# Retention and a gelu MLP on one core: earlier g sums, a seven-product first product from block 5 on, two more warm-ups and another hand-made order

## The chip, the cores and the metric

The kernel runs on one core of a Trainium2 chip. Its time is the device time of one execution in microseconds (us); lower is better. A core has TensorE (PE in the profile; PEld is its weight load), VectorE (DVE), ScalarE (ACT), GpSimd (POOL, which here only issues the load DMAs), SyncE (SP, which issues the stores and the transposing DMAs) and 16 DMA engines that all queues share.

## The reference

Retention for 8 batches, 8 heads, 576 positions and head size 64, then an MLP on the 4608 tokens that come out:

```python
scores = (q @ k.T) / sqrt(64)
Dmat[h] = where(i >= j, gamma_h ** (i - j), 0)      # gamma_h = 1 - 2 ** (-5 - h)
attn = (scores * Dmat) @ v                          # float32, [8, 8, 576, 64]
x = attn.transpose(0, 2, 1, 3).reshape(4608, 512)
h = x @ w_in                                        # 512 -> 2048
g = 0.5 * h * (1 + erf(h / sqrt(2)))
out = g @ w_out                                     # 2048 -> 512
```

Inputs and output are float32; the kernel multiplies in bfloat16.

## The kernel before, in words

**Attention.** Every batch is cut into five chunks of at most 128 positions (the fifth has 64), 40 chunks in all. For a chunk POOL loads q, k and v with a cast to bfloat16 (`load_chunk`, L247 and L251: from chunk 10 on, q and k go as two issues each). q and k are turned so that the head size lies on the partitions: the first 11 chunks with TensorE (`turn`, L343/L345, then a copy on DVE at L348 or ACT at L354), the others by a transposing DMA on SP (L332). A chunk then has: its v scaled by powers of gamma (`scaled_v`, DVE L432), scores on TensorE in 64 x 64 tiles (`together`, L382), a mask (`masked`: DVE L423 straight from PSUM, or ACT L421 first and then DVE), the inner product with v (`inner`, L458), a running state of the batch (`states`, L480 on TensorE, L489 to L498 on DVE and ACT), the cross product of q with that state (L382 again, into `o_ps`), and the write of x, transposed, by DVE (`evacuate`, L510). Work is done in groups: a group takes some *new* chunks up to their masked scores, and finishes the chunks that the group before had begun (the *held* ones). A chunk's x is therefore ready only with the group after its own.

**MLP.** Nine blocks of 512 tokens. Block t needs x of the chunks that cover its tokens: chunks 0 to 3 for block 0, to 8 for block 1, and so on for the later ones. Every block has a *first product* (h, then gelu on ACT into g) and a *second product* (g times w_out). All matmuls of both are issued at L320 (`product`). The tiles they write tell them apart in the profile: `hT` is the plain first product, 64 matmuls of 512 columns; `lean` is the first product by seven half-size products in place of eight (Strassen's scheme in Winograd's form), 4 groups x 7 x 4 matmuls of 256 columns; `fast` is the second product by seven products, 14 steps of 8 matmuls of 256 columns. A seven-product form needs sums of its operands beforehand: of g (`sum_g`, DVE L583 to L586, four slices S1 to S4 of a tile for each quarter of g), of w_out (`sum_weights`), of w_in (`sum_w_in`, L717 to L720, one of eight tiles at a time) and of x (`sum_x`, L734 to L737). And it combines the products: `lean` keeps two of them (L790 on ACT or L793 on DVE) and adds three times (DVE L797), before or between its gelus (L821).

`N_LEAN = 6` makes the first product of blocks 6, 7 and 8 `lean`; `N_DYN = 4` lets the first product of blocks 0 to 3 run on as many columns as have their x ("d" steps), while later blocks wait for all 512.

**The order.** No engine picks its work at run time. A planner in Python emits the instructions in one order for each engine, with a model clock for each engine, for PSUM banks and for the two DMA queues. It holds a list of *stages* and takes MLP steps only from the first stage that is not empty: first product of block 0; then first product of 1 with second of 0; then second of 1 with first of 2; and so on, and from the stage before the first `lean` block on, a lean first product together with the second product of the block before it. Between MLP steps it looks at what else can go (`attention_picks`): a group (G), scaling v (V), a turn (T), g sums (Z), late gelus (H), w_in sums (Y), x sums (X), w_out sums (W).

Groups come from `PLAN`. An entry is (number of new chunks, due, half-width). A group goes when `paced`, which counts 16 for each first or second product, has reached its due, or when the next MLP step is not ready for another 0.3 us of the model (*starved*). The third number says whether the full-array matmuls up to this group are issued as two half-width ones (`128*64` in the profile), so that the array need not change its tiling; two of these take the place of one `128*128`.

`LOADS` is the order in which POOL issues the first loads: a digit is a chunk (chunk 0 was loaded before), `i` the next of eight w_in tiles of 256 columns, `o` the next of eight w_out tiles. Afterwards chunk j + 10 is loaded when chunk j is done. w_in tile n serves rows 2n and 2n + 1 of the first product's 16. Other constants are margins of the planner: `V_SAFE` and `G_SAFE` (how long after the planned landing v is scaled, or a turned chunk is used), `Y_FROM` (from which `paced` on w_in sums may be made), `ACT_MASK` (how readily a mask goes by ACT), `T_LEAD`, `LAND_0`.

`sum_g` of block t is let go when the second product of block t - 1 has done 12 of its 14 steps, since the four slices are read up to then:

```python
if to_sum and fast_done.get(to_sum[0][0] - 1, 0) >= 12:
    got.append((g_ready(...) - 0.1, "Z", 0))
```

Before any MLP step is begun, the planner fills gaps of TensorE with matmuls of zeros (`warm`, L975); eight more stand at the very start (`warm_up`, L162).

Of the kernel before, what the change touches and what calls it, by code (L numbers as in the profile page):

```python
# [10 lines left out]
BF16 = mybir.dt.bfloat16  # L11
AF = mybir.ActivationFunctionType
ALU = mybir.AluOpType
# [3 lines left out]
def kernel(  # L17
# [14 lines left out]
    nc = tc.nc  # L32
# [11 lines left out]
    N_DF = d_ff // 128  # L44
# [6 lines left out]
    N_FIRST = 4  # L51
    N_LD = 7
    N_EX = 3
    Y_FROM = 88
    N_RING = 4
    LD_FIX = 2.0
    LD_TAIL = 1.7
    T_FIX = 2.1
    T_TAIL = 2.6
    T_DMA = 1.95  # L60
    N_DYN = 4
    N_LEAN = 6
    LEAN_FIRST = 1
    LOADS = "1 2 i 3 4 5 i 6 i i i 7 i i o i o o o 8 o o 9 o o"
    T_LEAD = 4
    V_SAFE = 4
    G_SAFE = 0
    TR_LEAD = 5
    POOL_0 = 1.05
    LAND_0 = (2.9, 4.15, 5.0)  # L70
    ACT_0 = 8.3
    COLS = ()
    CLOCK_0 = 3.2
    ACT_MASK = -0.2
    X_FROM = 10
    PLAN = [(1, 69, 1), (0, 67, 0), (0, 73, 0), (2, 142, 0), (1, 7, 1), (1, 119, 0), (2, 15, 0), (1, 61, 0), (2, 24, 0), (0, 26, 0), (0, 29, 0), (1, 0, 1), (2, 28, 0), (1, 58, 0), (2, 18, 0), (2, 29, 0), (0, 29, 0), (1, 21, 0), (2, 74, 0), (2, 99, 0), (2, 2, 0), (1, 47, 1), (2, 48, 0), (2, 106, 0), (2, 141, 1), (1, 154, 0), (2, 139, 0), (2, 69, 0), (2, 0, 1), (1, 68, 1), (0, 64, 1)]
    FAST_FROM = 0
    HALF = TOK_BLK // 2
    COL = d_model // 2
# [26 lines left out]
    clock = [0.0]  # L106
# [12 lines left out]
    def on_dve(ready, n, rate=1):  # L119
        return on("DVE", ready, n / rate / 960 + 0.072)  # L120
# [201 lines left out]
    def turn(i, parts=(0, 1)):  # L322

        cs = chunks[i][3]
        qk = loaded[i][0]
        s = st[i]
        if "qkT" not in s:
            s["qkT"] = tr_pool.tile([128, 2, HP, 128], BF16, tag="qkT", name="qkT")
            s["turned"] = 0.0
        qkT = s["qkT"]  # L330
        if i >= N_PE_TR:
            nc.sync.dma_start(qkT.rearrange("p j hp s -> p (j hp) s")[:, :, :cs],  # L332
                              qk[:cs].rearrange("p j h d -> p (j h d)"), transpose=True)
            transfer(1, clock[0] + T_FIX, T_DMA * cs / C, T_TAIL, s, "turned")
            return
        tiled(1 if by_col[0] and cs == C else 0)
        for j in parts:
            wait((land_q, land_k)[j][i] + 0.1)
            ps_, tag = bank([128, HP, 128], BF16, "qk_ps")
            for hp in range(HP):  # L340
                if by_col[0] and cs == C:
                    for e, sl in enumerate(HALVES):
                        nc.tensor.transpose(ps_[sl, hp, :cs], qk[:cs, j, 2 * hp + e, :], ident[:cs, :cs])  # L343
                else:
                    nc.tensor.transpose(ps_[:, hp, :cs], qk[:cs, j, 2 * hp:2 * hp + 2, :], ident[:cs, :cs])  # L345
            clock[0] += 0.23 * cs / C
            if i >= N_FIRST or i == 0:
                nc.vector.tensor_copy(qkT[:, j, :, :cs], ps_[:, :, :cs])  # L348
                end = on_dve(clock[0] + SEEN, HP * cs, 2)
                if i == 0 and j == 0:  # L350
                    nc.vector.tensor_scalar(msk[:, 0], row[:, :128], colp, None, op0=ALU.is_ge)
                    on_dve(end, 200)
            else:
                nc.scalar.copy(qkT[:, j, :, :cs], ps_[:, :, :cs])  # L354
                end = on_act(clock[0] + SEEN, HP * cs)
            free_at[tag] = end + BACK
            s["turned"] = max(s["turned"], end + BACK)
# [215 lines left out]
    w_sum_end = {0: 1e6, 4: 1e6}  # L573

    s_tiles = {}
    s_free = [0.0]

    def sum_g(t, n):

        g = g_tiles[t, n]  # L580
        a = {(r, c): g[:, :, c - 1, (r - 1) * HALF:r * HALF] for r in (1, 2) for c in (1, 2)}
        u = s_tiles[t, n] = s_pool.tile([128, 4, 2, HALF], BF16, tag=f"s{n}", name=f"s{n}")
        nc.vector.tensor_tensor(u[:, 0], a[2, 1], a[2, 2], op=ALU.add)  # L583
        nc.vector.tensor_tensor(u[:, 1], u[:, 0], a[1, 1], op=ALU.subtract)  # L584
        nc.vector.tensor_tensor(u[:, 2], a[1, 1], a[2, 1], op=ALU.subtract)
        nc.vector.tensor_tensor(u[:, 3], a[1, 2], u[:, 1], op=ALU.subtract)  # L586
        ready = max(s_free[0], g_ready(t, 0, TOK_BLK, range(4 * n, 4 * n + 4)))
        for x in range(4):
            s_end[t, n, x + 1] = on_dve(ready, 512, 2) + BACK

    def left(t, which, j, p):
# [343 lines left out]
    def attention_picks():  # L935
        got = []
        pend, i = held(), nxt["R"]
        pick = mlp_pick()
        kind, t = pick[1][0][:2] if pick is not None else ("s", N_BLK)
        starved = pick is None or pick[0] > clock[0] + 0.3  # L940

        if nxt["P"] < len(PLAN):
            size, due, _ = PLAN[nxt["P"]]
            new = list(range(i, i + size))
            if (paced[0] >= due or starved) and i + size <= nxt["T"]:
                got.append((group_ready(pend, new), "G", (pend, new)))
        i = nxt["V"]
        if i < nxt["T"] and i < nxt["S"] + 4:
            got.append((land_v[i] + (V_SAFE if i >= N_PE_TR else 0), "V", i))
        i = nxt["T"]  # L950
        if i < N_CH and i in land_v and i <= nxt["S"] + (T_LEAD if i < N_PE_TR else TR_LEAD):
            if i >= N_PE_TR:
                got.append((land_k[i], "T", i))
            elif i >= N_FIRST:
                got.append((max(land_k[i] + 0.1, banks_at(2)), "T", i))
            else:
                got.append((max((land_q, land_k)[half[0]][i] + 0.1, banks_at(1)), "T", i))
        if to_sum and fast_done.get(to_sum[0][0] - 1, 0) >= 12:
            got.append((g_ready(to_sum[0][0], 0, TOK_BLK, range(4 * to_sum[0][1], 4 * to_sum[0][1] + 4)) - 0.1, "Z", 0))
        if gelus:  # L960
            got.append((gelus[0][0] - 0.1, "H", 0))
        j = len(w_in_sums)
        if N_LEAN < N_BLK and j < len(w_in_sb) and not weights_due and paced[0] >= Y_FROM and nxt["S"] >= N_LD + N_EX:
            got.append((busy["DVE"] + 0.1, "Y", j))
        t = N_LEAN + len(x_sums)
        if t < N_BLK and j == len(w_in_sb) and (t == N_LEAN or lean_done.get(t - 1, 0) == 4 * len(FIRST_ORDER)) and x_ready(t * TOK_BLK, (t + 1) * TOK_BLK) < 1e5:
            got.append((max(busy["DVE"] + 0.1, x_ready(t * TOK_BLK, (t + 1) * TOK_BLK)), "X", t))
        if weights_due:
            got.append((weights_due[0][0], "W", 0))
        return got  # L970
# [6 lines left out]
    def attend(kind, i):  # L977
# [29 lines left out]
        elif kind == "V":  # L1007
            scaled_v(i)
            if i == 2:
                for t in ret_short + [vh_short]:  # L1010
                    nc.vector.memset(t, 0.0)
                    on_dve(clock[0], 256, 1.2)
            nxt["V"] += 1
        elif kind == "H":
            gelu_late()
        elif kind == "Y":
            sum_w_in(i)
        elif kind == "X":
            sum_x(i)
        elif kind == "Z":  # L1020
            sum_g(*to_sum.pop(0))
        elif kind == "W":
            sum_weights(*weights_due.pop(0)[1:])
        elif i < N_FIRST:
            turn(i, (half[0],))
            nxt["T"] += half[0]
            half[0] = 1 - half[0]
        else:
            turn(i)
            nxt["T"] += 1  # L1030
# [4 lines left out]
    def mlp(run):  # L1035
        step = run.pop(0)
        kind, t = step[:2]
        if kind == "d":
            m = step[2]
            lo, hi = reach(t, m)  # L1040
            if hi - lo < 64:
                hi = lo + 64
            done[t, m] = hi
            mlp1_step(t, m, lo, hi)
            cost = (hi - lo) / TOK_BLK
            if hi < TOK_BLK:
                run.append(step)
            else:
                for other in stages:
                    for r in other:  # L1050
                        if step in r:
                            r.remove(step)
        elif kind == "1":
            mlp1_step(*step[1:])
            cost = 1.0
        elif kind == "f":
            lean_step(*step[1:])
            lean_done[t] = lean_done.get(t, 0) + 1
            cost = 4.0 / len(FIRST_ORDER)
        else:  # L1060
            fast_step(t, step[2])
            fast_done[t] = step[2] + 1
            if step[2] == 11:
                s_free[0] = clock[0] + SEEN
            cost = 16 / len(FAST_ORDER)
        paced[0] += cost

# [51 lines left out]
```

## Time and profile before

| | |
|---|---|
| median of 6 runs | 289.58 us (288.21 to 291.76) |
| profiled execution | 289.64 us |
| its span, first to last instruction | 287.9 us |
| mean granted TensorE clock | 0.994 |
| POOL, which issues the loads, is last busy in | slice 26 of 40 (to 187 us) |
| first w_in sums / last | 108.6 us / 170.7 us |
| x sums of blocks 6, 7, 8 | 183.1, 213.1, 240.5 us |
| first second-product matmul | 50.47 us |
| last group of attention | 216.9 us |

The first lines of the page give each engine's busy time over the span, then the span in 40 slices of 7.2 us, where a digit is the busy share in tenths. An answer by stages gives, for each stretch, its length, the busy time of each engine with its number of instructions, the granted TensorE clock, the mean share of the DMA engines (over 1 when packets queue) and GB/s. The chain of waits runs from the last instruction back to what released it; its rows are start, length, engine, tile and number of instructions.

### The profile page before, as it was taken

To read this page: it belongs to the slowest core of one execution; us is meant where nothing else is said; L and a number is where in the kernel's file an instruction comes from. 1 tells how busy PE (TensorE), PEld (TensorE's weight loads), DVE (VectorE), ACT (ScalarE), POOL (GpSimd) and SP (SyncE) were. 2 spreads that over 40 slices of the span, in tenths; PEclk is the share of its full clock that TensorE was granted. 3 is DMA by queue.
4 is the path that set the end of the run, shared out by engine and by line. 5 is a ranking of instruction groups with operands and counts; after the bars stand their busy time and mean duration, and the time that the engine had idled before them with its cause. 6 is when DMAs were issued, how large, how long until landed. Compare 5 with 4: busy or idle time off the path is not lost.

```text
span 287.9 us, 8831 instructions
## 1 busy us (share of the span) xinstructions
PE 277.4 (96%) x3671; PEld 215.4 (75%) x3671; DVE 222.0 (77%) x553; ACT 152.2 (53%) x309; POOL 147.3 (51%) x198
## 2 busy tenths in 40 slices
PE   6769999999998999999999999999999999999995
PEld 2457557998887578656875588558999888888884
DVE  7888865874986895799779888998867965975552
ACT  3836576634425742576246723577662585467321
POOL 8987758998778369877968797300000000000000
PEclk9989999999999999999999999999999999999999
DMA  9999999999999999999999999990101210220223
GB/s 132 155 158 173 196 187 160 119 143 191 143 126 184 189 162 156 182 175 134 171 193 160 165 139 149 131 145 2 39 2 42 72 36 2 75 75 0 75 73 109
DMA packets 157319, 35.43 MB, mean 123 GB/s; under 512 B 141920, under 2 KB 157280, under 8 KB 157280
## 3 DMA queue, kind: packets, MB, share of 16 engines
q0 software_dynamic: 117792, 18.10, 96.3%
q1 hardware_dynamic: 39488, 16.78, 32.0%
q8 instruction: 28, 0.46, 0.7%
q14 instruction: 11, 0.09, 0.1%
HBM read 36.70 MB, written 9.44 MB: 160 GB/s over the span
## 4 chain that ended last, share of the span: by engine, by line
PE 89%; DMA 5%; POOL 3%; DVE 1%; issue 1%; ACT 0%; DVEq 0%; ACTq 0%; POOLq 0%
PE fast L320 37%; PE hT L320 30%; PE lean L320 13%; PE sc L382 3%; DMA qkT<-qk_ld 3%; PE o_ps L458 3%; DMA v_ld<-in_v_dram 2%; POOL qk_ld L251 2%; PE u_ps L480 2%; PE o_ps L382 1%; PE qk_ps L345 1%; POOL v_ld L251 1%; DVE ret L423 0%; POOL v_ld L128 0%; POOL w_in L262 0%
## 5 line engine op out<-in xcount | busy, mean ns | idle before, releaser
L320 PE MATMUL hT<-xT,w_in 128*64 128x512 bf16 (+8 forms) x624 | 88.9, 334 | 1.0 <-DVE xT L510 0.8
L320 PEld LDWEIGHTS <-w_in 128*128 128x128 bf16 (+1 forms) x816 | 62.8, 103 | 34.8 <-issue 1.0
L552 ACT ACTIVATE g<-hT 128x512 bf16<-128x512 f32 (+6 forms) x129 | 61.3, 490 | 30.7 <-PE hT L320 28.7
L320 PEld LDWEIGHTS <-s 128*128 128x128 bf16 (+1 forms) x616 | 56.5, 99 | 6.7 <-DVE s L584 0.3
L320 PE MATMUL fast<-w_sum,s 128*128 128x256 bf16 (+1 forms) x472 | 50.8, 273 | 0.0
L247 POOL DMA_DIRECT2D qk_ld<-in_q_dram x60 | 44.9, 777 | 11.4 <-DMA qkT<-qk_ld 8.1
L247 POOL DMA_DIRECT2D qk_ld<-in_k_dram x60 | 44.3, 761 | 10.0 <-DMA v_ld<-in_v_dram 6.0
L320 PEld LDWEIGHTS <-g 128*128 128x128 bf16 (+1 forms) x464 | 42.2, 100 | 5.5
L251 POOL DMA_DIRECT2D v_ld<-in_v_dram x39 | 35.0, 897 | 6.6 <-DVE o L675 1.8
L320 PE MATMUL fast<-w_out,g 128*128 128x256 bf16 (+1 forms) x320 | 33.4, 273 | 0.0
L671 ACT COPY u<-fast 128x512 f32<-128x512 f32 (+1 forms) x20 | 10.8, 542 | 37.0 <-PE fast L320 37.0
L675 DVE TENSOR_TENSOR o<-fast,u 128x512 f32<-128x512 f32 (+1 forms) x20 | 12.7, 633 | 19.4 <-ACT u L671 9.7
L510 DVE TENSOR_TENSOR xT<-o_ps,dq 128x256 bf16<-128x256 f32 (+1 forms) x84 | 26.5, 373 | 0.3 <-PE o_ps L382 0.3
L423 DVE TENSOR_TENSOR ret<-sc,msk 128x512 bf16<-128x512 f32 x39 | 25.0, 682 | 1.1 <-PE sc L382 0.8
L432 DVE TENSOR_TENSOR vh<-v_ld,dv 128x512 bf16<-128x512 bf16 x32 | 21.7, 680 | 1.8 <-DMA v_ld<-in_v_dram 1.8
L797 DVE TENSOR_TENSOR m<-lean,m 128x512 f32<-128x512 f32 x24 | 16.4, 687 | 6.8 <-PE lean L320 4.0
L583 DVE TENSOR_TENSOR s<-g 128x512 bf16<-128x512 bf16 x36 | 15.0, 417 | 5.2 <-ACT g L552 4.2
L382 PE MATMUL sc<-qkT 64*64 64x128 bf16 (+1 forms) x576 | 15.7, 218 | 1.6 <-DMA qkT<-qk_ld 0.9
L320 PE MATMUL fast<-w_sum,g 128*128 128x256 bf16 x144 | 17.2, 273 | 0.0
L320 PE MATMUL fast<-w_out,s 128*128 128x256 bf16 x144 | 17.2, 272 | 0.0
L821 ACT ACTIVATE g<-m 128x512 bf16<-128x512 f32 x24 | 14.9, 631 | 4.1 <-DVE m L797 4.1
L584 DVE TENSOR_TENSOR s<-s,g 128x512 bf16<-128x512 bf16 x36 | 15.3, 425 | 1.2
(93 smaller groups left out, 369.8 us busy)
## 6 DMA issues: line engine op xcount, KB each, us to landing
out_dram<-o SPq DMA_DIRECT2D x32, 256.0 KB, 4.2
v_ld<-in_v_dram POOLq DMA_DIRECT2D x32, 128.0 KB, 6.2
qk_ld<-in_q_dram POOLq DMA_DIRECT2D x50, 64.0 KB, 6.0
qk_ld<-in_k_dram POOLq DMA_DIRECT2D x50, 64.0 KB, 5.2
w_in<-in_moe_w_in_dram POOLq DMA_DIRECT2D x8, 256.0 KB, 8.2
w_out<-in_moe_w_out_dram POOLq DMA_DIRECT2D x8, 256.0 KB, 8.7
out_dram<-o SPq DMA_DIRECT2D x8, 128.0 KB, 1.7
qk_ld<-in_q_dram POOLq DMA_DIRECT2D x7, 128.0 KB, 6.0
```

The costliest lines, as they stand in the source:

```text
L247: nc.gpsimd.dma_start(dst[:cs, HP * odd:HP * odd + HP], src[b, odd::2, c0:c0 + cs, :].rearrange("h s d -> s h d"))
L251: nc.gpsimd.dma_start(dst[:cs], src[b, :, c0:c0 + cs, :].rearrange("h s d -> s h d"))
L320: nc.tensor.matmul(out_[sl], lhsT=lhsT[:, sl], rhs=rhs, start=start, stop=stop, skip_group_check=True)
L382: nc.tensor.matmul(out_, lhsT=lhsT, rhs=rhs, start=start, stop=stop, skip_group_check=True)
L423: nc.vector.tensor_tensor(r[:cs, :, :cs], src, msk[:cs, :, :cs].to_broadcast([cs, HP, cs]), op=ALU.mult)
L432: nc.vector.tensor_tensor(vh[:cs], loaded[i][1][:cs], dv[:cs, :, ci:ci + 1].to_broadcast([cs, H, D]), op=ALU.mult)
L510: nc.vector.tensor_tensor(xT[:, g::2, at:at + hi - lo], s["o_ps"][g][:, s["place"], :, lo:hi], dq[:, g::2, c0 + lo:c0 + hi], op=ALU.mult)
L552: nc.scalar.activation(g_of(t, m, lo, hi), hT[:, :hi - lo], AF.Gelu)
L583: nc.vector.tensor_tensor(u[:, 0], a[2, 1], a[2, 2], op=ALU.add)
L584: nc.vector.tensor_tensor(u[:, 1], u[:, 0], a[1, 1], op=ALU.subtract)
L797: nc.vector.tensor_tensor(dst, acc_, f[to], op=ALU.add)
L821: nc.scalar.activation(g_tile(t, n)[:, :, r - 1, lo:lo + HALF], src, AF.Gelu)
```

## The change

- `sum_g` is split: the sums into slices 1, 2 and 3 of block t are let go after 10 steps of the second product of t - 1 (those slices are read in steps 5 to 10), the one into slice 4 after 12 steps, by a new pick "E" that comes ahead of "Z". The four sum tiles are allotted once and no longer taken anew from a pool for each block.
- `N_LEAN` goes from 6 to 5, `N_DYN` from 4 to 3.
- Two warm-up matmuls of 512 columns are issued after chunk 0's q is turned.
- `LOADS`, `PLAN` and the margins are other ones.

```diff
-    Y_FROM = 88
+    Y_FROM = 20
...
-    N_DYN = 4
-    N_LEAN = 6
+    N_DYN = 3
+    N_LEAN = 5
     LEAN_FIRST = 1
-    LOADS = "1 2 i 3 4 5 i 6 i i i 7 i i o i o o o 8 o o 9 o o"
-    T_LEAD = 4
-    V_SAFE = 4
-    G_SAFE = 0
+    LOADS = "1 i 2 3 4 5 6 i i 7 i i i 8 i i 9 o o o o o o o o"
+    T_LEAD = 5
+    V_SAFE = 1
+    G_SAFE = 0.5
...
-    LAND_0 = (2.9, 4.15, 5.0)
+    LAND_0 = (2.9, 4.3, 5.0)
...
-    ACT_MASK = -0.2
+    ACT_MASK = 0.3
     X_FROM = 10
-    PLAN = [(1, 69, 1), (0, 67, 0), (0, 73, 0), (2, 142, 0), (1, 7, 1), (1, 119, 0), (2, 15, 0), (1, 61, 0), (2, 24, 0), (0, 26, 0), (0, 29, 0), (1, 0, 1), (2, 28, 0), (1, 58, 0), (2, 18, 0), (2, 29, 0), (0, 29, 0), (1, 21, 0), (2, 74, 0), (2, 99, 0), (2, 2, 0), (1, 47, 1), (2, 48, 0), (2, 106, 0), (2, 141, 1), (1, 154, 0), (2, 139, 0), (2, 69, 0), (2, 0, 1), (1, 68, 1), (0, 64, 1)]
+    PLAN = [(1, 528, 0), (1, 321, 0), (1, 269, 1), (2, 27, 0), (2, 99, 0), (2, 135, 0), (1, 17, 0), (1, 4, 1), (1, 19, 0), (1, 0, 0), (2, 24, 0), (2, 48, 0), (1, 43, 0), (1, 32, 1), (2, 85, 0), (2, 39, 0), (2, 22, 0), (2, 52, 0), (2, 125, 0), (0, 109, 0), (1, 77, 0), (2, 27, 0), (0, 82, 1), (1, 128, 1), (1, 112, 0), (1, 81, 1), (1, 124, 1), (0, 6, 1), (2, 160, 1), (2, 56, 1), (0, 71, 1)]
...
                 if i == 0 and j == 0:
+                    warm(2)
                     nc.vector.tensor_scalar(msk[:, 0], row[:, :128], colp, None, op0=ALU.is_ge)
...
-    s_free = [0.0]
-
-    def sum_g(t, n):
+    s_free = [0.0, 0.0]
+    to_end = []
+
+    s_sb = [s_pool.tile([128, 4, 2, HALF], BF16, name=f"s{n}") for n in range(N_DF // 4)]
+
+    def sum_g(t, n, last):
...
-        u = s_tiles[t, n] = s_pool.tile([128, 4, 2, HALF], BF16, tag=f"s{n}", name=f"s{n}")
+        u = s_tiles[t, n] = s_sb[n]
+        if last:
+            nc.vector.tensor_tensor(u[:, 3], a[1, 2], u[:, 1], op=ALU.subtract)
+            s_end[t, n, 4] = on_dve(s_free[1], 512, 2) + BACK
+            return
...
-        nc.vector.tensor_tensor(u[:, 3], a[1, 2], u[:, 1], op=ALU.subtract)
         ready = max(s_free[0], g_ready(t, 0, TOK_BLK, range(4 * n, 4 * n + 4)))
-        for x in range(4):
+        for x in range(3):
...
-        if to_sum and fast_done.get(to_sum[0][0] - 1, 0) >= 12:
+        if to_end and fast_done.get(to_end[0][0] - 1, 0) >= 12:
+            got.append((clock[0], "E", 0))
+        if to_sum and fast_done.get(to_sum[0][0] - 1, 0) >= 10:
             got.append((g_ready(to_sum[0][0], 0, TOK_BLK, range(4 * to_sum[0][1], 4 * to_sum[0][1] + 4)) - 0.1, "Z", 0))
...
-            sum_g(*to_sum.pop(0))
+            to_end.append(to_sum[0])
+            sum_g(*to_sum.pop(0), False)
+        elif kind == "E":
+            sum_g(*to_end.pop(0), True)
...
-            if step[2] == 11:
-                s_free[0] = clock[0] + SEEN
+            if step[2] in (9, 11):
+                s_free[step[2] // 11] = clock[0] + SEEN
```

## The prediction

> **What bounds the kernel now.** I read the page first (busy shares, then the slices), then the busy time by stage, then the chain, then the first 43 us on TensorE, VectorE and the load queue.
>
> ```profile
> PE 277.4 (96%) x3671; PEld 215.4 (75%) x3671; DVE 222.0 (77%) x553; ACT 152.2 (53%) x309; POOL 147.3 (51%) x198
> PE   6769999999998999999999999999999999999995
> DVE  7888865874986895799779888998867965975552
> PEclk9989999999999999999999999999999999999999
> DMA  9999999999999999999999999990101210220223
> ```
>
> TensorE is busy everywhere but in the first three slices (7.2 us each) and in slice 13; the DMA engines are full for the first 27 slices. So the end is the start-up, plus TensorE's work, plus a tail. Stages (PE, PEld, DVE, ACT, POOL busy, clock, DMA share, GB/s):
>
> ```profile
> 9.00:19.20 10.20, 6.47 (x163) 4.52 (x162) 8.36 (x20) 6.57 (x15) 9.46 (x13) 1.00 2.29 157
> 19.20:27.15 7.95, 7.82 (x141) 6.32 (x140) 6.90 (x19) 3.43 (x11) 7.05 (x9) 0.79 1.80 172
> 27.15:43.00 15.85, 15.85 (x134) 8.80 (x132) 12.22 (x32) 11.00 (x22) 10.25 (x14) 1.00 1.65 188
> 60.00:100.00 40.00, 39.13 (x517) 31.40 (x515) 29.94 (x70) 17.18 (x37) 30.14 (x41) 1.00 1.90 163
> 165.00:197.00 32.00, 32.00 (x465) 22.33 (x465) 27.43 (x72) 15.94 (x31) 15.68 (x22) 1.00 1.46 129
> ```
>
> From 19.2 us on TensorE stands still for 0.13 + 0.87 us, and 0.13 more near 250 us. The 0.87 is one wait for a DMA transpose at 88.0 us. The clock of 0.79 in the second row is one record of half clock, 19.39 to 22.80 us, with TensorE busy: about 1.7 us lost. The chain gives prices per matmul, and VectorE shows what the start hangs on:
>
> ```profile
> 266.35 18.35 PE fast L320 x168
> 204.12 7.04 PE lean L320 x128
> 187.74 7.03 PE hT L320 x64
> ```
> ```profile
> 11.89 0.69 DVE L432 TENSOR_TENSOR vh<-v_ld,dv 128x512 bf16<-128x512 bf16 x1 [1.03 <-DMA v_ld<-in_v_dram]
> 16.61 0.69 DVE L432 TENSOR_TENSOR vh<-v_ld,dv 128x512 bf16<-128x512 bf16 x1 [0.80 <-DMA v_ld<-in_v_dram]
> ```
>
> 18.35/168 = 109.2 ns for 256 columns. The 64 hT rows are half-width pairs: 7.03/32 = 0.220 us for 512 columns; at full width the chain has 28 in 6.04 us, 0.2157 each. VectorE stands waiting for the v of chunk 2 and of chunk 3: start-up is paced by landings, one about every 0.9 us.
>
> **The Trainium skill.** TensorE: Matmul & The Clock Gate, "What's actually happening": the array runs at half clock after a window of some 3.4 us with little activity. The trace agrees: the half-clock record is 3.413 us long and follows a stretch where TensorE was busy 6.47 of 10.20 us. Same page, "Wait — 56ns, not 53.3ns?": N/2.4 + 2.5 ns, 109.2 ns at 256 columns; the trace has 109.2. VectorE: DVE Perf Modes, "The perf-mode tier table": tensor_tensor runs at double rate on bf16 in SBUF, at single rate with float32 or PSUM; here 418 ns (s) against 687 ns (m<-lean,m), both of 512 columns.
>
> **The change, part by part.**
>
> *Seven products for block 5.* Out go 64 matmuls of 512 columns, 64 x 0.2157 = 13.80 us. In come 4 groups x 7 products x 4 matmuls of 256: 112 x 0.1092 = 12.23. TensorE: -1.6 us (-1.8 if the old ones ran half-width). It lies on the path, as TensorE never rests there. Beside it VectorE gains 12 adds x 0.69 = 8.3 and four x sums x 0.418 = 1.7; the 8 keeps go to ACT mostly (20 of 24 did), 8 x 0.59 = 4.7 there.
>
> *Is VectorE cover enough?* By counting units before it (16 per product), block 5's first product would share its stage with block 4's second, from about 165 us. That stage has VectorE at 27.43 of 32.00. Of the eight w_in sums (4 x 0.285 = 1.1 us each) two stand here, at 169.8 and 170.7 us; they move to before 70 us, where VectorE has room: -2.3. The four x sums at 183 stay, for block 5 in place of 6. 27.4 - 2.3 + 8.3 = 33.4 us in some 30.4: over by 3.0. The mask constant moves masks to ACT (414 ns on VectorE in place of 682): a third of some 9 saves 0.8. The rest can be put off until after 197 us, where VectorE is at 16.21 of 20.00. Bounds: 0 to +3; I take +0.3.
>
> *The g sums.* Same four operations, 36 of each at 418 ns; only their start moves. Waits for fast matmuls before L583 are 1.0 us in three, on VectorE, and weight loads wait 0.3 us for s in all. TensorE has other products while they run: 0, bounds -0.3 to +0.3.
>
> *Two warm-ups.* They fall between 5.24 and 6.23 us, where TensorE waits 1.00 us for k's cast; at 0.43 us each they need 0.86. Cover gone, +0.4; taken 0.
>
> *Safety margins.* v may be scaled 3 us sooner after its planned landing. From chunk 11 on, where the margin holds, VectorE scales v at the least 2.0 us after it landed (chunk 12, at 62.5 us), else at the least 4.0 (chunks 20, 21, 28): one wait of 1 us may come on VectorE, with masks and x queued behind it, while TensorE has matmuls that need neither; 0, upper bound +1. A group of attention waits 0.5 us longer for its transposes: the 0.87 us stall at 88.0 may go, or come back elsewhere. -0.4, bounds -0.9 to +0.5.
>
> *Load order.* Bytes are unchanged and the last w_out lands at 50.2 us either way, so the first second product (at 50.47) keeps its start; POOL has the same issues, and from chunk 10 on the loads follow as before. In between I shift the landings of before by what goes ahead: chunk 2.8 us, w_in tile 1.3. w_in 0: 13.4 to 10.4; chunk 2: 11.9 to 13.3; chunk 3 stays at 16.6; w_in 1 (the second): 21.9 to 25.5; w_in 3 and 4 +2.5 us, 6 +2.5, 7 +1.2; chunk 6 lands 1.4 earlier, 7 and 8 about 2.7 and 8. Block 1's first product can't begin before block 0's is whole, since the planner looks at the first stage alone. So until 25.5 us TensorE has from weights only w_in 0: 2 x 0.87 us.
>
> *The list there.* New groups are chunks 1; 2; 3+4; 5+6; 7+8; 9. A chunk's x comes with the next group. x of chunk 2 thus waits for chunk 4 (landed 18.7), x of chunk 3, which completes block 0, for chunk 6 (24.2): about 27 us, against 19.5 to 24 now. TensorE from 19.5 to 25.3 then has group 3+4 (1.2 us), a 128-column piece of two tiles (0.4), transposes of 5 and 6 (0.9), half of group 5+6 (0.8): 3.3 of 5.8 us, idle 2.5. From 25.5 on, tiles 2 to 5 with the rest of 0 and 1 and chunk 7's transposes fill up to 29.9; w_in 3 lands at 30.7: idle 0.8. Tiles 6 to 11 fill up to 36; w_in 6 lands at 37.3, less chunk 8's transposes: idle 0.8. Together 4.1. Credit: 0.4, as one more 128-column piece falls before 19 us; and the half clock of before, 1.7 us, would lie under idle time now, but can return when work resumes: I take half, 0.8. +2.9, bounds -1.7 (other attention fills every hole and the clock does not drop) and +5.4 (no clock credit, and one half-clock window of 3.4 us on resumed work).
>
> *Other.* 31 list entries each; two more do something (31 against 29), at some 0.3 us; three more half-width stretches save as many switches. 0.
>
> Sum: 287.9 - 1.6 + 0.3 - 0.4 + 2.9 = 289.1 span. The profiled execution took 289.64, 1.7 outside its span: 290.8. Its time stands 0.06 above the median of the runs, so 290.8 is also the forecast against 289.58: +0.4%.
>
> **Rivals.**
> A, the forecast: the early hole eats the saving. 290.8; its own range 287.7 to 292.4.
> B, slower: half clock on the resumed work. Place: 25.5 to 30 us. The window before it has TensorE busy about half, less than the stretch that brought the dip of before. Price: early term +5.4 for +2.9, 293.3. It decides once the early loss passes 4.6 us. Against: the warm-ups at 5 us don't reach it, but TensorE's many small matmuls count too, and the stretch 9 to 16 us had no dip.
> C, faster: the hole is filled. Attention of chunks 5 and 6 done singly is not in the list, but its pieces may be spread; no dip; the 0.87 goes. -1.6 - 0.9 - 1.7 = -4.2: 285.4. Against: before 25.5 us one w_in tile is there and nothing else can be multiplied.
> D, VectorE becomes the bound from 165 to 197: +3.0 in place of 0.3, 293.5; if half is made up after, 292. For: 33.4 in 30.4. Against: the second product of block 4 (12.2 us) asks VectorE for only three adds and is there to fill.
> That the change does not do what it says I leave at nothing: the first product of a block is one of two forms, and 5 is named.
>
> **How the numbers follow.** A 0.58, all within 1%. B 0.22, all slower. C 0.10: 0.09 faster, 0.01 within. D 0.10: half slower, half within. About 1% (2.9 us) is what a measurement here can tell from nothing. Faster 0.09, same 0.64, slower 0.27. Range: A's lower end, set a little down for C's nearest part, 287.2, up to B and most of D, 294.0; left out are most of C and the far ends. A's own range stands above.
>
> **What would show it.** In the new profile: lean matmuls 448 full-width equivalents, not 336, and hT 320 for 384; TensorE's busy time between 19.2 and 43 us down by 2 to 4 us, with idle before w_in tiles or chunk 6's transposes; w_in sums before 70 us; the last group of attention near 217 us less 1.6 plus the early loss; fast from 266 us on unchanged. A half-clock record after 25 us speaks for B; VectorE over 95% from 165 to 197 with TensorE waiting for m or s speaks for D. I am wrong if TensorE is as full at 19 to 43 us as now, or if new idle time stands in the middle.

## The result, and the profile after

The changed kernel takes 290.15 us (median of 34 runs, 288.67 to 292.65), the kernel before 289.28 us (69 runs beside it, 287.13 to 293.27). The ratio is 1.0041, 95% interval 1.0027 to 1.0055: 1.2 us slower, where 290.8 against 289.58, also 1.2 us, was forecast. The profiled execution took 289.66 us with a span of 287.9, as long as that of the kernel before (289.64 and 287.9), so these two executions don't show the difference: that of the kernel before lies 0.4 us above its median, that of the changed kernel 0.5 us under its own. What they show, stage by stage, is where the saving is spent again.

The page after, busy shares and slices:

```profile
PE 278.8 (97%) x3992; PEld 220.8 (77%) x3992; DVE 231.0 (80%) x575; ACT 155.5 (54%) x311; POOL 147.2 (51%) x198
PE   8779999999999999999999999999999999999995
DVE  7699687688957896899959799599789877997732
PEclk9986999999999999999999999999999999999999
DMA  9999999999999999999999999942202101120223
```

VectorE has 9.0 us more, close to the 9.2 that the prediction's terms add up to (8.3 + 1.7 - 0.8). TensorE looks fuller in slices 1 and 3. In slice 1 stand the two new warm-ups; in slices 3 and 4 its clock has an 8 and a 6. The same stages as before:

```profile
9.00:19.20 10.20, 7.09 (x146) 4.81 (x146) 7.48 (x18) 6.58 (x15) 9.99 (x13) 1.00 2.70 152
19.20:27.15 7.95, 7.33 (x145) 6.12 (x140) 7.43 (x19) 2.81 (x8) 7.14 (x10) 0.57 2.33 166
27.15:43.00 15.85, 15.85 (x176) 9.28 (x175) 12.24 (x33) 11.22 (x25) 11.87 (x17) 1.00 1.63 189
60.00:100.00 40.00, 39.86 (x527) 30.27 (x527) 32.10 (x82) 16.08 (x32) 31.55 (x43) 1.00 2.01 168
165.00:197.00 32.00, 32.00 (x496) 28.56 (x494) 26.98 (x60) 21.33 (x42) 15.06 (x21) 1.00 1.42 130
```

In the second row the clock is 0.57: the record has half clock from 19.75 to 26.58 us, two windows where the kernel before had one. TensorE is "busy" for 7.33 of 7.95 us there because the little it has takes twice as long. The mean clock hides idle time, and busy time hides half clock, so I counted work instead: every matmul that has begun, at the measured prices (109.2 ns for 256 columns, 215.7 ns for 512, and on the straight line through these two for other widths), halved for half-width and quartered for 64 x 64 tiles, warm-ups left out. The *lag* is the time less the work begun until then, that is, what TensorE has lost so far to waits, to half clock and to small pieces. What the seven products save is no part of the lag; it is in the total of the work:

| at us | lag before | lag after | after less before |
|---|---|---|---|
| 19.2 | 14.60 | 14.48 | -0.1 |
| 27.15 | 17.11 | 18.86 | +1.8 |
| 43 | 17.81 | 19.62 | +1.8 |
| 80 | 19.94 | 21.61 | +1.7 |
| 100 | 22.07 | 22.75 | +0.7 |
| 165 | 24.93 | 26.37 | +1.4 |
| 197 | 26.51 | 27.74 | +1.2 |
| 284 | 27.45 | 29.06 | +1.6 |

The work itself fell by 1.72 us: hT 83.2 to 69.3, lean 36.7 to 48.9, all else as before. So the changed kernel has 1.7 us less to do, and is 1.8 us behind from its start-up on. What it regains from 80 to 100 us is mostly one wait of the kernel before that it doesn't have:

```profile
88.00 0.42 PE L382 MATMUL sc<-qkT 64*64 64x128 bf16 x16 [0.87 <-DMA qkT<-qk_ld]
```

The chain gives the same prices as before: 109.2 ns for 256 columns at full width, 54.5 ns at half width, and 219 ns for 512 columns, where the kernel before, too, has a row of 32 in 7.01 us:

```profile
268.86 15.73 PE fast L320 x144
206.49 4.80 PE lean L320 x88
128.23 7.01 PE hT L320 x32
```

VectorE's longest early wait is no longer for v of chunk 2 or 3, but for scores; the v's have landed when it comes to them. Chunk 2's v landed at 13.34 us and is scaled at 16.87, so it is the list that holds it up:

```profile
11.93 1.29 DVE L424 TENSOR_TENSOR ret<-sc,msk 128x512 bf16<-128x512 f32 x2 [1.45 <-PE sc L383]
16.87 0.68 DVE L433 TENSOR_TENSOR vh<-v_ld,dv 128x512 bf16<-128x512 bf16 x1
18.29 0.63 DVE L433 TENSOR_TENSOR vh<-v_ld,dv 128x512 bf16<-128x512 bf16 x1
```

### The profile page after: what moved, and what is told of

Same layout as the page of the kernel before. It is cut to its first block, busy times and chain, and to the rows that moved or that the text cites. A ratio compares the mean times of both kernels' runs of the same rounds, so it can differ in the third digit from the quotient of the medians.

```text
span 287.9 us, 9521 instructions
## 1 busy us (share of the span) xinstructions
PE 278.8 (97%) x3992; PEld 220.8 (77%) x3992; DVE 231.0 (80%) x575; ACT 155.5 (54%) x311; POOL 147.2 (51%) x198
## 4 chain that ended last, share of the span: by engine, by line
PE 86%; DVE 8%; ACT 3%; DMA 1%; issue 1%; SPq 0%; DVEq 0%; ACTq 0%
PE fast L320 36%; PE hT L320 22%; PE lean L320 17%; PE sc L383 3%; PE o_ps L459 3%; PE u_ps L481 2%; DMA k<-in_k_dram 1%; PE o_ps L383 1%; DVE xT L511 1%; DVE ret L424 1%; ACT dq L169 1%; DVE s L588 1%; PE qk_ps L345 1%; DVE vh_short L433 1%; DVE s L592 1%
## 5 line engine op out<-in xcount | busy, mean ns | idle before, releaser
L320 PEld LDWEIGHTS <-w_in 128*128 128x128 bf16 (+1 forms) x764 | 56.8, 104 | 33.2 <-DVE xT L511 1.7
L320 PE MATMUL hT<-xT,w_in 128*128 128x512 bf16 (+8 forms) x468 | 73.8, 343 | 1.4 <-DVE xT L511 1.3
L553 ACT ACTIVATE g<-hT 128x512 bf16<-128x512 f32 (+4 forms) x99 | 49.8, 517 | 22.6 <-PE hT L320 21.7
L804 DVE TENSOR_TENSOR m<-lean,m 128x512 f32<-128x512 f32 x32 | 21.8, 686 | 5.4 <-PE lean L320 4.7
L828 ACT ACTIVATE g<-m 128x512 bf16<-128x512 f32 x32 | 20.1, 631 | 8.7 <-DVE m L804 8.5
L424 DVE TENSOR_TENSOR ret<-sc,msk 128x512 bf16<-128x512 f32 x30 | 19.7, 684 | 3.2 <-PE sc L383 2.3
L496 ACT CAST u_sb<-run_sum 128x256 bf16<-128x256 f32 x24 | 9.7, 405 | 22.7 <-DVE run_sum L493 17.8
L320 PEld LDWEIGHTS <-w_in_sum 128*64 128x64 bf16 (+1 forms) x288 | 20.2, 106 | 1.4 <-issue 0.2
L320 PE MATMUL lean<-x_sum,w_in_sum 128*64 128x256 bf16 (+1 forms) x216 | 19.9, 273 | 0.0
L422 ACT CAST ret<-sc 128x512 bf16<-128x512 f32 x34 | 18.3, 585 | 2.7 <-PE o_ps L383 2.7
```

Source lines behind the costliest of these rows:

```text
L320: nc.tensor.matmul(out_[sl], lhsT=lhsT[:, sl], rhs=rhs, start=start, stop=stop, skip_group_check=True)
L422: nc.scalar.copy(r[:cs, :, :cs], src)
L424: nc.vector.tensor_tensor(r[:cs, :, :cs], src, msk[:cs, :, :cs].to_broadcast([cs, HP, cs]), op=ALU.mult)
L553: nc.scalar.activation(g_of(t, m, lo, hi), hT[:, :hi - lo], AF.Gelu)
L804: nc.vector.tensor_tensor(dst, acc_, f[to], op=ALU.add)
L828: nc.scalar.activation(g_tile(t, n)[:, :, r - 1, lo:lo + HALF], src, AF.Gelu)
```

## The experiments

The theories: (1) the early feed of w_in and the pairing of chunks eat what the seven products save; (2) the half clock costs the time; (3) VectorE can't carry block 5's extra adds, and the saving is given back as waits. Ratios are against runs of the kernel before on the same chip, with 95% intervals.

**The load order of before in the changed kernel** (`after_loads_before`).
```diff
-    LOADS = "1 i 2 3 4 5 6 i i 7 i i i 8 i i 9 o o o o o o o o"
+    LOADS = "1 2 i 3 4 5 i 6 i i i 7 i i o i o o o 8 o o 9 o o"
```


> The changed kernel with the load order of before. If the early feed of w_in is what eats the saving (theory 1), useful TensorE work by 43 us rises by about half of the 1.8 us that it lies behind, since the list of groups still pairs chunks 3+4 and 5+6: 289.2 us against 290.15. If the half clock alone costs the time (theory 2), it stays within 0.4 us unless the granted clock rises. If VectorE in the lean stage is the cause (theory 3), 290.1.


297.37 us, ratio 1.0305 (1.0268 to 1.0342): a miss, but a telling one. At 35 us the lag is 16.50, 2.4 us better than in the changed kernel (at full clock here, which was worth 1.1 at 27 us) and 1.3 better than before (17.79, with one half-clock window): this load order does feed TensorE. Then the list asks for chunks 7 and 8 together, and chunk 8 now lands after four w_out tiles. TensorE's waits from 35 to 50 us:

```profile
40.44 0.40 PE L345 MATMUL qk_ps<-ident,qk_ld 128*128 128x128 bf16 x4 [2.88 <-DMA qk_ld<-in_q_dram]
41.20 0.61 PE L345 MATMUL qk_ps<-ident,qk_ld 128*128 128x128 bf16 x4 [0.37 <-DMA qk_ld<-in_k_dram]
45.56 0.29 PE L345 MATMUL qk_ps<-ident,qk_ld 64*128 64x64 bf16 x4 [1.03 <-DMA qk_ld<-in_q_dram]
46.46 0.29 PE L345 MATMUL qk_ps<-ident,qk_ld 64*128 64x64 bf16 x4 [0.61 <-DMA qk_ld<-in_k_dram]
```

Two half-clock windows, from 40.86 and 47.69 us, come with these waits. At 60 us it lags by 26.51, 5.9 us worse than the changed kernel. List and load order are one decision.

**The load order of the changed kernel in the kernel before** (`before_loads_after`), the same edit the other way.


> The kernel before with the load order of the changed one alone. Theory 1, early feed: useful TensorE work at 27 us falls back by about 1.5 us, as in the changed kernel (1.75), and stays lost: 290.6 to 291.3 against 288.9. If it is the pairing of chunks in the list that costs the time, not the loads: 289.3 or less.


296.41 us, ratio 1.0256 (1.0212 to 1.0300). At 27 us it lags 1.0 us more than before, at 43 us 2.3 more (20.11 against 17.81): an early loss comes with the loads alone, though the old list takes chunks 3 and 4 singly. How much of it is half clock is not separated here: the run has two windows, from 15.58 to 22.41 us, where the kernel before has one. The rest comes at 94.5 us, where TensorE waits 3.3 us for a DMA transpose, probably again a list that doesn't fit its loads; the total is thus no measure of the early step.

**Block 5 by seven products alone** (`before_lean5`).
```diff
-    Y_FROM = 88
+    Y_FROM = 20
-    N_LEAN = 6
+    N_LEAN = 5
```


> The kernel before with the seven-product first product from block 5 on, and its w_in sums let go from 20 units of work on; nothing else. Theory 1: it saves what TensorE saves, 1.7 us, so 287.6 against 289.3. Theory 3: VectorE can't keep up from 165 to 197 us, TensorE waits for m or s, and the time stays at 289.3 or goes over it.


298.36 us, ratio 1.0356 (1.0317 to 1.0394). Up to 197 us nothing is given back: its lag is 24.95 against 26.51 of the kernel before, even 1.6 us less. (This is not the saving, which the lag leaves out; the wait at 88 us, 0.87 us, is gone here.) Then it loses 12 us until 255. TensorE's waits from 214 to 256 us in its timeline:

```profile
224.76 4.78 PE L320 MATMUL fast<-w_sum,s 128*64 128x256 bf16 x84 [1.78 <-DVE s L584]
239.78 1.92 PE L320 MATMUL lean<-x_sum,w_out 128*64 128x256 bf16 x16 [3.50 <-DVE x_sum L736]
252.83 0.60 PE L320 MATMUL lean<-x_sum,w_in_sum 128*128 128x256 bf16 x4 [1.63 <-DVE lean L797]
```

These waits are 6.9 us of it, and a half-clock window from 239.23 us comes with the longest. VectorE is not full (16.93 of 23.00 us from 217 to 240): it comes late with what TensorE asks for next. The last group of attention, at 217 us before, comes at 246 here, so x of the last blocks, and the x sum at 238.5 us, come when the seven-product steps already wait for them. The old list doesn't hold for the new mix of work: TensorE does wait for VectorE, as theory 3 says, though not because VectorE lacks time.

**Block 5 plain again in the changed kernel** (`after_lean6`).
```diff
-    N_LEAN = 5
+    N_LEAN = 6
```


> The changed kernel with block 5's first product plain again, list and all else kept. If the seven products save TensorE's 1.7 us under this list (theory 1), it comes out 1.7 us slower than the changed kernel: 291.8. If they give back what they save as waits for VectorE (theory 3), it stays at 290.1.


292.12 us, ratio 1.0127 (1.0095 to 1.0158), against 1.0041 for the changed kernel: 2.5 us slower, 1.5 to 3.5 by the two intervals. In the profile its lag at 284 us is 28.90 (changed kernel 29.06), so up to there nothing but the work differs, by 1.72 us, and TensorE's last matmul ends 1.4 us later (285.99 against 284.58). Another 1.4 us of this one execution is its last store, which landed 3.12 us after its issue, in the changed kernel 1.70. Under its own list the saving is real and is not given back: theory 3 falls for the changed kernel.

**All four g sums after 12 steps** (`after_sums_whole`).
```diff
-        if to_sum and fast_done.get(to_sum[0][0] - 1, 0) >= 10:
+        if to_sum and fast_done.get(to_sum[0][0] - 1, 0) >= 12:
```


> The changed kernel with its first three g sums let go after 12 steps of the second product of the block before, as the fourth, and not after 10. The prediction's step says 0, 0.3 at most: 290.1. If the seven products of block 5 leave so little room on VectorE that the sums must be early (theory 3), TensorE waits for s or m between 190 and 240 us and several us are lost, 294 or more.


298.98 us, ratio 1.0371 (1.0337 to 1.0404). At 180 us it is 1.7 us ahead of the changed kernel (lag 24.95 against 26.62), at 240 it is 8.3 behind. VectorE's timeline, then TensorE's:

```profile
197.60 0.43 DVE L592 TENSOR_TENSOR s<-s,g 128x512 bf16<-128x512 bf16 x1
197.95 0.42 DVE L593 TENSOR_TENSOR s<-g 128x512 bf16<-128x512 bf16 x1
198.28 0.42 DVE L588 TENSOR_TENSOR s<-g,s 128x512 bf16<-128x512 bf16 x1
198.62 0.42 DVE L490 COPY run_sum<-u_ps 128x256 f32<-128x256 f32 x1
```
```profile
199.09 3.14 PE L320 MATMUL fast<-w_out,g 128*64 128x256 bf16 x30 [3.58 <-DVE run_sum L490]
```

From 192.77 to 198.62 us VectorE makes sixteen sums in a row. Behind them stands the copy of the running state out of PSUM (L490), and the next second product, which needs no sum at all, waits for it: 3.58 us. That the two share a PSUM bank is inferred from this wait; the records do not name banks. A second wait, 2.70 us for an addition of the output on VectorE, follows at 225.6, and half-clock windows from 198.41 and 229.13 us come with the two. The time is the one expected under theory 3, but the waits are not for `s` or `m`: what VectorE does is in the wrong order for TensorE. In the changed kernel twelve sums run from 192.50 to 197.01 and the last four, apart, from 198.68; there TensorE has no wait in this stretch.

**The split alone in the kernel before** (`before_split_sums`): the diff of the change in `sum_g` and its picks, nothing else.


> The kernel before with the split of the g sums alone: three after 10 steps, the fourth after 12, sum tiles allotted once. The prediction's step says 0, 0.3 at most: 288.6 to 289.3. If starting the sums earlier puts them ahead of masks and x on VectorE that attention waits for, 290 to 291.


290.51 us, ratio 1.0083 (1.0054 to 1.0112), slower by more than the changed kernel, and in the range expected if the early sums stand ahead of what attention needs. It has a wait of the same kind in another place, at 70.6 us:

```profile
72.48 2.69 PE L320 MATMUL fast<-w_out,g 128*128 128x256 bf16 x23 [1.88 <-DVE run_sum L492]
```

It also gives a pair: neither this profile nor that of `after_sums_whole` has a half-clock record before 190 us. At 43 us their lags are 16.14 and 18.72, so with the old and the new start compared at full clock, the new one is 2.6 us behind. Here the busy time shows the hole as well, first the old start (`before_split_sums`), then the new one (`after_sums_whole`):

```profile
19.20:27.15 7.95, 7.85 (x147) 5.83 (x146) 7.74 (x22) 4.94 (x14) 7.93 (x11) 1.00 1.83 176
```
```profile
19.20:27.15 7.95, 6.09 (x149) 4.60 (x144) 7.92 (x21) 3.49 (x10) 7.33 (x10) 1.00 2.22 166
```

TensorE stands idle for 1.9 us in this stretch with the new start and for 0.1 with the old one; from 27.15 to 43 us both are full. `after_loads_before` makes a third: it has the new list and the old loads, and no half clock before 40 us. At 27.15 us the three lags are 15.60 (old), 16.59 (new list, old loads) and 17.72 (new), at 35 us 16.06, 16.50 and 17.79. So the loads make 1.1 of 2.1 us and then 1.3 of 1.7, and the rest is the list's with its margins, in one execution each.

**Filled gaps** (`after_warm_fill`, `before_warm_fill`).
```diff
-        if gap > 0.4 and not mlp_begun[0]:
+        if gap > 0.28 and (not mlp_begun[0] or clock[0] < 25):
```


> The changed kernel with TensorE's planned gaps of over 0.28 us before 25 us of the planner's clock filled with matmuls of zeros, also after the first MLP step. Theory 1: the half clock lies mostly under idle time, so at most 0.4 us is won: 289.8 to 290.2. Theory 2: no half-clock window after 20 us, granted clock 1.0, and 1.2 us or more is won: 288.9.


289.74 us, ratio 1.0037 (1.0019 to 1.0054).


> The kernel before with the same filling. Its half-clock window at 19.4 to 22.8 us falls on busy TensorE, so if filling removes it: granted clock 1.0 and 1.2 to 1.7 us less, 287.6 to 288.1. If the gaps that stay (waits that the planner does not foresee) are what drops the clock: 289.3 and clock 0.994.


289.01 us, ratio 1.0011 (0.9992 to 1.0029). The filling does what it should to the clock in the profiles; over all executions it does so in the kernel before (21 of 22 at a clock of 0.998 or more), in the changed kernel in 6 of 17 only. First the changed kernel filled, then the kernel before filled, 19.20 to 27.15 us:

```profile
19.20:27.15 7.95, 7.75 (x170) 5.47 (x164) 7.92 (x21) 3.48 (x10) 7.05 (x10) 1.00 1.94 155
```
```profile
19.20:27.15 7.95, 7.84 (x148) 5.79 (x147) 7.63 (x21) 4.04 (x13) 7.80 (x10) 1.00 1.73 163
```

The changed kernel's lag at 27 us falls by 1.1, at 43 us by only 0.3: a row of first products that began at 40.54 us begins at 40.24, after a wait for chunk 9's k. At the end 0.2 is left, and the time falls by nothing that the intervals hold. The kernel before gains nothing either, though a window there was priced at 1.2 to 1.7 us: a miss. The filling seems to cost something itself: at a clock of 0.998 or more, on the same chip, the kernel before has a median of 289.06 us filled (21 runs) and 287.75 unfilled (12). So these two runs don't decide on theory 2. What speaks against it as the main cause is the pair above, 2.6 us apart at full clock.

**Without the two warm-ups** (`after_no_warm2`): `warm(2)` taken out.


> The changed kernel without its two new warm-up matmuls. The prediction's step: 0, 0.4 at most: 289.7 to 290.5. If they keep the clock up (theory 2), the granted clock falls in more executions and it is 0.6 to 1.2 us slower.


290.86 us, ratio 1.0066 (1.0047 to 1.0084), 0.7 us slower than the changed kernel by the two ratios, with overlapping intervals. Of its 22 runs 13 have a granted clock under 0.990, of the changed kernel's 34 nine. They seem to keep a half-clock window away now and then; it is not settled.

**New lists** (`mixed_list1`, `mixed_list2`, `mixed_list1_fill`): the changed kernel with other lists, load orders and margins (`N_DYN` is 4 again in the first), meant to be ahead by the planner's own model clock, whose times are not on record here. Of the first, the load order:
```diff
-    LOADS = "1 i 2 3 4 5 6 i i 7 i i i 8 i i 9 o o o o o o o o"
+    LOADS = "i 1 2 3 i 4 i 5 6 i i 7 i i i o 8 o o o o 9 o o o"
```


> The changed kernel (block 5 by seven products, split g sums, two warm-ups) with a new list of groups and an order of loads that alternates chunks and w_in tiles, 1 2 3, then a w_in tile after nearly every chunk. Theory 1: without the early hole the changed form keeps what the seven products save: useful TensorE work at 43 us is as before or better, and the time is 1 to 2 us under before, 286.5 to 288. If the seven products can't hold their saving in any list (theory 3): 289 to 290.

> As the one before with a second new list, w_in tiles after chunks 3, 5 and 6. Theory 1: 286.8 to 288.3; theory 3: 289 to 290.

> The first of these with TensorE's early gaps filled with matmuls of zeros. If half clock still costs something where TensorE is busy: clock 1.0 and 0.4 to 1.2 us under the first. If it lies under idle time: no difference within 0.4 us.


291.12 us, ratio 1.0078 (1.0054 to 1.0101); 291.78, 1.0103 (1.0070 to 1.0136); 293.44, 1.0140 (1.0099 to 1.0182). All three miss, and the first one filled is 2.3 us slower than unfilled. The first one's TensorE timeline:

```profile
29.31 1.05 PE L320 MATMUL hT<-xT,w_in 128*64 128x512 bf16 x7
32.47 1.89 PE L320 MATMUL hT<-xT,w_in 128*64 128x512 bf16 x15 [2.11 <-issue]
```

The profile names nothing that ended this wait. A w_in tile lands at 32.61 us by its load's record, so it is likely that the step waited for the tile and that the planner, having put the step there, had counted on it sooner. At 43 us the lag is 20.57, worse than the changed kernel's 19.62. A list picked for the least model time may be picked for the model's errors too. So no version here beats the kernel before.

## Why the prediction was right, point by point

The mechanism came as forecast: the seven products save 1.7 us of work, and a hole before block 0's x is complete costs about as much. That the sum came out at the same 1.2 us is partly luck. The early term was 1.8 us in the profiled executions where 2.9 was forecast, and the -0.4 for the margins rests on a wait that goes without them too. The two profiled executions add up to -1.7 + 1.6 = -0.1 us, where the ratio over all runs says +1.2 (0.8 to 1.6).

One sign that the prediction named for itself failed: TensorE's busy time from 19.2 to 43 us, to fall by 2 to 4 us, went from 23.67 to 23.18, because half clock counts as busy. At full clock, in the pair of starts above, it is 23.70 and 21.94, 1.8 us less.

- *Seven products, -1.6.* Right: 1.72 us of work, and `after_lean6` loses 1.5 to 3.5 us without it. What the prediction did not say is that the saving needs a list made for it: with the old one it is lost several times over.
- *VectorE cover, 33.4 us of work in 30.4 from 165 to 197.* Wrong as a picture, harmless in the sum. VectorE has 26.98 of 32.00 there. The work went later: 46.10 us in the stretch from 217 us on became 53.08. The prediction kept the last group of attention near 217 us; it comes at 245. Also, w_in sums were to be over before 70 us; they run from 60.8 to 142.7, wherever VectorE is free.
- *g sums, 0 (-0.3 to +0.3).* The step failed in its reason: "TensorE has other products while they run" looked at who reads the sums, not at what is queued behind them on VectorE. Whole, they cost this list 8.8 us by medians (9.5 by the ratios); split, they cost the old list 2.3 us by medians. What the term is in the changed kernel itself is not shown: no list made for whole sums was run beside its own.
- *Warm-ups, 0.* Not settled: without them it is 0.7 us slower, with overlapping intervals.
- *Margins, -0.4.* From 80 to 100 us the changed kernel regains 1.0 us of lag, 0.87 of it the wait for a transpose at 88 us that is gone. By 165 us it has lost 0.8 of this again. But the wait is gone as well in `before_lean5`, `before_split_sums` and `before_warm_fill`, which keep the old margins. So it is not shown that the margins removed it, and what they do stays open.
- *Load order and list, +2.9.* Landings came as worked out: w_in 0 at 10.45 (10.4), chunk 2 at 13.34 (13.3), w_in 1 at 25.25 (25.5), w_in 3 at 29.80 (30.7), w_in 6 at 36.68 (37.3), chunk 6 at 23.46 (24.2). Block 0's x was complete when forecast, just after 27 us. The loss is 1.8 us in the profiled executions, 2.6 at full clock in the pair above. The holes at 29.9 and 36 us, 0.8 each, did not come; one reason is that tiles land 0.6 to 0.9 us sooner than I had put them. The first second product did not keep its start: it comes at 58.83 us, not at 50.47. TensorE has other products until then and does not wait.
- *The half clock credit, 0.8.* It came, as far as one profile each can tell. At 43 us the kernel before lags 17.81 with its one window and 16.14 without any (`before_split_sums`, whose matmuls have the same order until 74 us); the changed kernel lags 19.62 with its two and 18.72 without any (`after_sums_whole`). So the window costs the kernel before 1.7 us and the two cost the changed one 0.9. From 19.20 to 27.15 us the changed start leaves TensorE idle for 1.9 us without them and for 0.6 with them: they lie partly under what was idle time. The medians by granted clock are looser. The changed kernel has 289.83 (full, 6 runs), 290.12 (0.994, one window, 17) and 291.31 (0.988, two, 7). For the kernel before, one window is worth 1.4 us on one chip (287.82 full, 9 runs; 289.19 at 0.994, 14) and 0.9 on another (288.14, 11; 289.00, 12).
- *The rivals.* B had its windows, but they ended at 26.58 us, as work resumed. C did not come, since the hole was not filled. D did not come: VectorE is busy for 84% of the stretch from 165 to 197 us.

What stays open is why all runs show 1.2 us where the two profiled executions show none, what the warm-ups and the margins do, and why the filled kernel before gains nothing by medians. No run gives the changed kernel a better start and leaves the rest of it whole, so that the early hole makes up the 1.2 us is argued from the lags, not shown by a run.

## What to carry to other kernels

A kernel with a hand-made order is not a sum of edits: in the kernel before, the load order, block 5's form and the split of the sums each cost 2 to 10 us when moved alone (7.4, 10.3 and 2.4 by the ratios), and 1.2 together, with a list of their own. Read a changed order by the work done until fixed times, since a busy share counts half clock as work. And for a step moved on an engine that works in the order of its queue, ask what stands behind it there; here it was the copy of the running state out of PSUM.

## What the runs showed of the hardware

By the granted clock, TensorE's half-clock windows differ in number between executions of the same program (none, one or two in the changed kernel, in 6, 17 and 7 of 34 runs). A half-clock window need not cost half its length: the two of the changed kernel (6.83 us) raise its lag at 27 us by 1.1 us, against both `after_warm_fill` and `after_sums_whole` (18.86 against 17.72).

Before five half-clock records later on (40.86 us in `after_loads_before`, 97.50 in `before_loads_after`, 198.41 and 229.13 in `after_sums_whole`, 239.23 in `before_lean5`) TensorE was busy for only 0.46 to 0.73 of 3.41 us; each comes with a wait of 2.7 us or more. A sixth, at 47.69 us, follows 1.77 us of busy time, and a wait of 2.73 us in `mixed_list1_fill` has none after it. Such a wait can cost more than its own length: from 80 to 100 us the lag grows by 6.2 us in `before_loads_after` and by 2.1 in the kernel before, with waits of 3.5 and 0.9 us. In the start-up no such border can be read: the kernel before was busy for 1.99 us from 12.56 to 15.97 and kept full clock, and for 2.02 us in the next 3.42 and lost it. The prediction's "the trace agrees" holds for the length of the record, then, and not for how little activity it takes.

Half-width pairs run the seven-product steps at the price of full width (88 in 4.80 us, 54.5 ns each), for twice as many weight loads.
